# A two-layer linear-attention and gated-MLP kernel on one core: the key weights' transposing load first in SyncE's queue, X's first tile at the head of ScalarE's, and a new order of the operations

## The chip, the cores and the metric

The kernel runs on one core of a Trainium2 chip. Its time is device microseconds of one execution, as the median of three runs: 388.36 us before the change (388.30 to 389.07). Lower is better. The engines are named as in the profile: PE (TensorE, matmuls), PEld (its weight loads), DVE (VectorE), ACT (ScalarE), POOL (GpSimd) and SP (SyncE, which only issues DMAs here). DMAs are issued by SP, whose queue is q1 in the profile, and by ACT, whose queue is q10.

## What is computed

x has 2048 rows of 512 values. The reference applies the same two blocks twice: linear attention with 32 heads of 16, then a gated MLP of width 1376, each on a layer norm of x and added to x.

```python
qkv = x @ wqkv                                  # q, k, v: 32 heads of 16
pq = einsum("bhsd,hdf->bhsf", q, w_phi)         # and pk from k
phi_q = concat([softmax(pq), softmax(-pq)])     # and phi_k from pk
kv = einsum("bhsf,bhsd->bhfd", phi_k, v)
z = einsum("bhsf->bhf", phi_k)
o = (phi_q @ kv) / (phi_q @ z + 1e-6)
x = x + o @ wo                                  # on layernorm(x)
x = x + (relu(gate) * up) @ W_down              # gate, up on layernorm(x)
```

## The kernel before

x stays in SBUF as X, 16 tiles of 128 rows, four tiles to a chunk. For each tile of the first layer norm DVE takes statistics (`bn_stats`, L311, and `bn_aggr`, L313), POOL makes the scale and the bias from them (L319 to L370), ACT, DVE or POOL normalises (L382 or L394), and the result is turned, so that the 512 columns lie on partitions: by a DMA that transposes, issued by SP (L412 for one tile, L408 for two), or by PE (L403) with a copy out of PSUM (L405). Tile 0 is turned by PE in layer 0.

The weights of q and k are folded with w_phi once (`feature_weights`): wkT, the key weights turned, comes by one transposing DMA straight out of DRAM (L169). DVE spreads w_phi into Wblk (L269), PE multiplies (four folds of four matmuls, L287), and ACT and DVE copy the four results into Wk2 (copies are recorded at L249 for ACT and L251 for DVE). The query weights follow later in the same way (their turn is L279 on SP).

Then comes, for each tile of a chunk, the key stage: the key product on PE (L575), two exponentials on ACT (L580), the value product (L516) with its copy to vext, sums over the features on DVE (L546 to L556, partly with POOL, L532), a reciprocal (L589), the scaling on POOL or DVE (L595), and the product that gathers kv and z in PSUM (L617, cleared first by L610). Queries go the same way (L659, L663, L670, L674, L681) and end in a transposing DMA (L683). Attention multiplies by R (L700, built on DVE at L639), divides (L718, L720), turns by PE (L740) or DMA, projects with wo (L751) and adds to X (L420). The MLP is L446 to L498.

PE also runs 18 "wake" matmuls of zeros (L260) whose result nobody reads; where they stand is part of the order.

Nothing is scheduled at run time. `Plan` collects some 1860 operations with a planned cost, and `ORDER` is a list that gives the sequence in which they are emitted; each engine runs its own operations in that sequence and waits where an operand or a buffer isn't ready. `STEP` holds, by characters, which engine does an operation of a tile, and in which form. `WF_IN`, `WK_IN`, `WV_IN`, `WQ_IN` and `X_IN` are the planner's guesses of when the first loads land; they enter only its own arithmetic, by which buffer slots are assigned, and are no waits.

The first loads are issued in `setup` ahead of the plan: SP issues X's tile 0 (L168) and the turn of the key weights (L169); ACT issues w_phi (L170), X's tile 1 (L171), tiles 2 and 3 (L172), then the value weights wvt (L179) and the rest of X (L180 to L182).

Of the kernel before, what the change touches and what calls it, by code (L numbers as in the profile page):

```python
# [133 lines left out]
WF_IN, WK_IN, WV_IN, WQ_IN, LOADED = 3.35, 6.0, 8.3, 13.0, 13.0  # L134
X_IN = [3.1, 4.7] + [6.8] * 2 + [9.8] * 4 + [11.3] * 4 + [12.8] * 4
# [8 lines left out]
def setup(ctx, tc, A_x, A_wqkv, A_w_phi, A_wo, B_W_gate, B_W_up, B_W_down, out):  # L144
    nc = tc.nc
# [16 lines left out]
    X = const.tile([P, T, D], BF16, name="X")  # L162
    xv = xf.rearrange("(t p) d -> p t d", p=P)
# [4 lines left out]
    nc.sync.dma_start(out=X[:, 0:1, :], in_=xv[:, 0:1, :])  # L168
    nc.sync.dma_start_transpose(out=wkT[:], in_=A_wqkv[:, D:2 * D])  # L169
    nc.scalar.dma_start(out=wf[:], in_=A_w_phi.rearrange("(b j) d f -> (j d) b f", b=NDB, j=8))  # L170
# [517 lines left out]
def attention(st, c, pT, norm, L):  # L688
# [257 lines left out]
```

## Time and profile before

| | us |
|---|---|
| median of three runs | 388.36 |
| the profiled execution | 387.81 |
| its span in the trace | 386.1 |
| PE busy in the span | 369.1 |
| DVE busy | 277.5 |
| ACT busy | 195.5 |
| POOL busy | 133.7 |

The span runs from the first to the last recorded instruction. In rows of the timeline the columns are start, duration, engine, line, operation, output and inputs, count, and in brackets the engine's idle time ahead of it with what ended that. In the chain of work that ended last they are start, duration and what. In busy time by stretch they are the stretch, its length, the busy time of PE, PEld, DVE, ACT and POOL with the number of instructions, the granted PE clock as a share, the DMA engines' busy share and GB/s. In rows of a DMA queue they are packets, MB and the time that the packets took as a share of 16 engines.

### The profile page before, as it was taken

How to read it: one execution, taken by the hardware profiler on the slowest of the kernel's cores; microseconds unless marked ns; L12 is line 12 of the kernel's file. 1: busy time of each engine (PE TensorE's matmuls, PEld its weight loads, DVE VectorE, ACT ScalarE, POOL GpSimd, SP SyncE). 2: the span in 40 equal slices, each digit the busy share in tenths (PEclk: the TensorE clock that was granted, in tenths of full speed). 3: DMA queues.
4: the chain of work that ended last, by engine and by line, in shares of the span. 5: the costliest groups of instructions: out<-in, count | busy, mean ns of one | idle time of the engine just before them, and what ended most of it. 6: DMA issues, size and time to landing. Idle time of an engine off the chain costs nothing.

```text
span 386.1 us, 6719 instructions
## 1 busy us (share of the span) xinstructions
PE 369.1 (96%) x2412; PEld 191.1 (49%) x2412; DVE 277.5 (72%) x606; ACT 195.5 (51%) x418; POOL 133.7 (35%) x273
## 2 busy tenths in 40 slices
PE   4799999999989999999999999999999999999997
PEld 1345454666544554444454445476545445444444
DVE  5599999999858786466659878989974565423432
ACT  2689967934456621225876456896443714032100
POOL 4489885832542100053315253451622211000000
PEclk9599999999999999999999999999999999999999
DMA  8679585735582440014203132464793330201004
GB/s 182 186 125 213 136 242 110 124 64 95 112 129 54 83 69 15 0 28 86 48 6 68 28 44 41 82 121 76 129 156 65 67 59 4 54 14 56 0 5 133
DMA packets 100673, 31.95 MB, mean 83 GB/s; under 512 B 92096, under 2 KB 100640, under 8 KB 100640
## 3 DMA queue, kind: packets, MB, share of 16 engines
q1 hardware_dynamic: 97584, 29.02, 38.7%
q10 hardware_dynamic: 3056, 2.51, 2.3%
q8 instruction: 19, 0.31, 0.3%
q14 instruction: 14, 0.11, 0.1%
HBM read 7.39 MB, written 2.10 MB: 25 GB/s over the span
## 4 chain that ended last, share of the span: by engine, by line
PE 75%; DVE 13%; DMA 6%; ACT 2%; issue 2%; POOL 1%; SPq 0%; POOLq 0%
PE ps L466 34%; PE ps L498 17%; PE ps L751 6%; PE ps L659 4%; PE ps L575 4%; DMA b<-b 4%; PE ps L516 3%; PE ps L446 2%; DMA wkT<-in_A_wqkv_dram 2%; DVE sk L556 2%; DVE rk L589 2%; DVE sk L546 2%; DVE sq L546 2%; PE q L700 2%; DVE b L595 1%
## 5 line engine op out<-in xcount | busy, mean ns | idle before, releaser
L476 ACT CAST b<-ps 128x512 bf16<-128x512 f32 (+2 forms) x100 | 47.8, 503 | 99.5 <-PE ps L466 94.4
L466 PE MATMUL ps<-b,wg 128*128 128x512 bf16 (+2 forms) x400 | 79.6, 336 | 0.0
L498 PE MATMUL ps<-wd,b 128*128 128x512 bf16 (+4 forms) x374 | 79.6, 366 | 0.0
L466 PE MATMUL ps<-b,wu 128*128 128x512 bf16 (+2 forms) x400 | 78.8, 336 | 0.0
L479 DVE SCALAR_TENSOR_TENSOR b<-ps,b 128x512 bf16<-128x512 f32 (+2 forms) x70 | 39.9, 604 | 27.7 <-PE ps L466 13.9
L595 POOL TENSOR_TENSOR b<-b,rk 128x1024 bf16<-128x1024 bf16 (+7 forms) x29 | 40.1, 1396 | 43.1 <-ACT b L476 13.1
L498 PEld LDWEIGHTS <-b 128*128 128x128 bf16 (+1 forms) x374 | 35.2, 98 | 38.7
L466 PEld LDWEIGHTS <-wu 128*128 128x128 bf16 x400 | 36.0, 98 | 33.0 <-issue 0.3
L466 PEld LDWEIGHTS <-wg 128*128 128x128 bf16 x400 | 35.9, 98 | 31.4
L424 DVE TENSOR_TENSOR X<-X,ps 128x512 bf16<-128x512 bf16 (+2 forms) x34 | 22.1, 653 | 33.4 <-PE ps L498 23.4
L580 ACT ACTIVATE b<-ps 128x512 bf16<-128x512 f32 x64 | 36.3, 646 | 10.1 <-PE ps L575 10.1
L382 ACT ACTIVATE b<-X,ve,rstd 128x512 bf16<-128x512 bf16 x39 | 32.1, 834 | 15.8 <-POOL ve L370 14.4
L663 ACT ACTIVATE b<-ps 128x512 bf16<-128x512 f32 x64 | 34.2, 615 | 10.7 <-PE ps L659 10.5
L575 PE MATMUL ps<-Wk,b 128*128 128x512 bf16 x128 | 32.9, 387 | 4.4 <-DMA b<-b 2.4
L516 PE MATMUL ps<-wvt,b 128*128 128x512 bf16 x128 | 32.5, 384 | 0.4 <-ACT vext L249 0.4
L751 PE MATMUL ps<-wo,b 128*128 128x512 bf16 x128 | 31.5, 379 | 0.4 <-DMA b<-b 0.4
L681 POOL TENSOR_TENSOR b<-b,rq 128x512 bf16<-128x512 bf16 x23 | 24.6, 1070 | 19.1 <-DVE rq L674 15.6
L659 PE MATMUL ps<-Wq,b 128*128 128x512 bf16 x128 | 30.9, 379 | 0.0
L334 ACT ACTIVATE sq<-X 128x512 bf16<-128x512 bf16 x32 | 20.3, 635 | 18.6 <-DVE X L420 18.4
L420 DVE SCALAR_TENSOR_TENSOR X<-ps,X 128x512 bf16<-128x512 f32 x32 | 21.6, 678 | 5.9 <-PE ps L498 5.1
L341 POOL TENSOR_SCALAR u<-mv 128x2 f32<-128x2 f32 (+1 forms) x20 | 4.6, 234 | 55.8 <-DVE X L420 55.4
L546 DVE TENSOR_REDUCE sq<-b 128x64 f32<-128x1024 bf16 x20 | 23.7, 1201 | 0.0
(86 smaller groups left out, 461.1 us busy)
## 6 DMA issues: line engine op xcount, KB each, us to landing
out_dram<-X SPq DMA_DIRECT2D x15, 128.0 KB, 1.8
X<-in_A_x_dram ACTq DMA_DIRECT2D x3, 512.0 KB, 9.5
b<-b SPq DMA_TRANSPOSE x95, 3.1
wd<-in_B_W_down_dram SPq DMA_DIRECT2D x5, 256.0 KB, 3.3
wu<-in_B_W_up_dram SPq DMA_DIRECT2D x8, 160.0 KB, 3.9
wg<-in_B_W_gate_dram SPq DMA_DIRECT2D x8, 160.0 KB, 3.1
wvt<-in_A_wqkv_dram ACTq DMA_DIRECT2D x1, 512.0 KB, 7.4
wo<-in_A_wo_dram SPq DMA_DIRECT2D x4, 128.0 KB, 3.6
```

The lines of the kernel that those rows point to most:

```text
L466: nc.tensor.matmul(ps[:], lhsT=wt[:, b, f * P:(f + 1) * P], rhs=xnT[:, lo:hi, b, :], start=(b == 0), stop=(b == NDB - 1))
L476: pl.op("ACT", 0.065 + 0.42 * share, lambda ups=ups, ru=ru: nc.scalar.copy(out=ru[:], in_=ups[:]), reads=[(ups, 0)], writes=[(ru, 0)])
L479: pl.op("DVE", 0.08 + 0.53 * share, lambda gps=gps, ru=ru, h=h, cs=cs: nc.vector.scalar_tensor_tensor(out=h[:, cs], in0=gps[:], scalar=0.0 ...
L498: nc.tensor.matmul(yps[:], lhsT=hs[f][:fsz, ti * P:(ti + 1) * P], rhs=st.wd[:fsz, f, cols], start=(f == 0), stop=(f == NFT - 1))
L516: nc.tensor.matmul(vp[:], lhsT=xnT[:, ti, kb, :], rhs=st.wvt[:, kb, :], start=(kb == 0), stop=(kb == NDB - 1))
L546: pl.op("DVE", 1.13, lambda: nc.vector.tensor_reduce(out=sums[:].rearrange("p j s h -> p (j s) h"), in_=e[:].rearrange("p j s (f h) -> p ( ...
L575: nc.tensor.matmul(ps[:], lhsT=xnT[:, ti, kb, :], rhs=w(kb), start=(kb == 0), stop=(kb == NDB - 1))
L580: pl.op("ACT", 0.49, lambda s=s, ek=ek, pk=pk: nc.scalar.activation(out=ek[:, :, s, :], in_=pk[:].rearrange("p (j x) -> p j x", j=8), func ...
L595: eng.tensor_tensor(out=phiK[:, lo:hi, :, :].rearrange("p j s (f h) -> p (j s) f h", h=4), in0=ek[:, lo:hi, :, :].rearrange("p j s (f h) - ...
L659: nc.tensor.matmul(pq[:], lhsT=xnT[:, ti, kb, :], rhs=st.Wq2[:, kb, :], start=(kb == 0), stop=(kb == NDB - 1))
L663: pl.op("ACT", 0.49, lambda s=s, eq=eq, pq=pq: nc.scalar.activation(out=eq[:, :, s, :], in_=pq[:].rearrange("p (j x) -> p j x", j=8), func ...
L751: nc.tensor.matmul(yps[:], lhsT=turned(b), rhs=st.wo[:, b, :], start=(b == 0), stop=(b == NDB - 1))
```

## The change

The two loads on SP become one, and X's tile 0 goes to ACT's queue, ahead of w_phi. The planner's landing times are set anew. Three characters of `STEP` change. `ORDER` is a new list; it has two operations fewer (1861), because with tile 14's second layer norm on DVE (in "xB0") two small POOL operations that fed ACT are not needed. "qs0" moves the scaling of tile 9's query features in layer 0 from DVE to POOL.

```diff
-WF_IN, WK_IN, WV_IN, WQ_IN, LOADED = 3.35, 6.0, 8.3, 13.0, 13.0
-X_IN = [3.1, 4.7] + [6.8] * 2 + [9.8] * 4 + [11.3] * 4 + [12.8] * 4
+WF_IN, WK_IN, WV_IN, WQ_IN, LOADED = 5.5, 5.7, 8.25, 13.0, 13.0
+X_IN = [3.1, 6.0] + [6.75] * 2 + [9.75] * 4 + [11.25] * 4 + [12.75] * 4
...
-    nc.sync.dma_start(out=X[:, 0:1, :], in_=xv[:, 0:1, :])
     nc.sync.dma_start_transpose(out=wkT[:], in_=A_wqkv[:, D:2 * D])
+    nc.scalar.dma_start(out=X[:, 0:1, :], in_=xv[:, 0:1, :])
     nc.scalar.dma_start(out=wf[:], in_=A_w_phi.rearrange("(b j) d f -> (j d) b f", b=NDB, j=8))
...
-    "sB1": 3, "sA": 3, "xB0": "ADADDADDDADADDAD", "xB1": "DADAAADDDAAAADAA", "xA": "AADDDDDAAAAAAAAA",
-    "xm0": "21122111", "xmB0": "12222112", "xmB1": "22222221", "xm1": "11222212", "om0": "11112222",
+    "sB1": 3, "sA": 3, "xB0": "ADADDADDDADADDDD", "xB1": "DADAAADDDAAAADAA", "xA": "AADDDDDAAAAAAAAA",
+    "xm0": "21122111", "xmB0": "22222112", "xmB1": "22222221", "xm1": "11222212", "om0": "11112222",
...
-    "qm1": "DDDDPPDDDDPDDPDD", "qr0": "1111H1122121P1PP", "qr1": "1112112122111112", "qs0": "PPPPPPPPDDDPDPPP",
+    "qm1": "DDDDPPDDDDPDDPDD", "qr0": "1111H1122121P1PP", "qr1": "1112112122111112", "qs0": "PPPPPPPPDPDPDPPP",
```

The lists of `ORDER` are not printed. Engine by engine the sequence differs up to the first attention tiles of layer 0 and is the same behind them but for the two moved operations. What the text on record speaks of:

| engine | before | after |
|---|---|---|
| PE, start | 12 wakes, folds 3, 1, 0, 2, turn of tile 0, keys 0, 3 wakes, values 0, L610, keys 1, values 1 | 8 wakes, folds 3, 0, wake, turn of tile 0, fold 2, wake, fold 1, keys 0, 2 wakes, values 0, 4 wakes, L610, values 1, keys 1 |
| ACT, start | copies of folds 0, 1, 2, normalise tile 1, copy of the turned tile 0, normalise 2, 3, exponentials of tile 0 | copies of fold 0, turned tile 0, folds 2, 1, normalise tiles 1, 2, exponentials of tile 0, normalise 3 |
| DVE, ahead of the first key sum (L556, tile 0) | statistics of tiles 0 to 8 | of tiles 0 to 7; tile 2's ahead of the copy of fold 3 |
| DVE, ahead of the sum of tile 1 (L546) | statistics of tiles 0 to 11, 13, 15 | and of tile 14; the aggregate of tile 15 comes later |
| DVE, ahead of the first L720 | 104 operations | the same and one reciprocal of tile 5 (L670) |
| PE, ahead of the first L740 | 94 operations | the same and L700 of tile 1 |
| SP, behind the turn of tiles 6 and 7 | turn of tiles 8 and 9, then weight loads | two weight loads, then the turn of tiles 8 and 9 |

186 rows, old and new, of the table ORDER are left out of this document.

## The prediction

> **What bounds the kernel now.** I read the page first, then busy time by stretch, then the chain of work that ended last, then the timeline of single engines. The page and the stretches say where time can be won at all:
>
> ```profile
> span 386.1 us, 6719 instructions
> PE 369.1 (96%) x2412; PEld 191.1 (49%) x2412; DVE 277.5 (72%) x606; ACT 195.5 (51%) x418; POOL 133.7 (35%) x273
> ...
> 0.00:20.00 20.00, 12.27 (x47) 5.46 (x48) 11.33 (x34) 8.94 (x14) 9.61 (x35) 0.74 0.75 178
> 20.00:40.00 20.00, 19.69 (x123) 9.48 (x121) 19.77 (x40) 18.72 (x36) 18.30 (x24) 1.00 0.85 172
> 40.00:60.00 20.00, 18.68 (x175) 10.27 (x174) 20.00 (x38) 16.18 (x33) 16.98 (x13) 1.00 0.71 186
> ...
> 120.00:160.00 40.00, 40.00 (x215) 19.49 (x214) 28.95 (x54) 14.71 (x30) 4.05 (x10) 1.00 0.24 40
> ```
>
> PE is busy 369.1 of 386.1 us; 7.7 us of its 17.0 idle us lie in the first 20. From 20 to 60 DVE is full (19.77 and 20.00 of 20), so there DVE sets the pace. From 120 on it is PE alone. The chain says the same with the places:
>
> ```profile
> 1.24 9.20 DMA wkT<-in_A_wqkv_dram
> ...
> 10.48 1.47 PE ps L287 x12
> ...
> 14.73 0.05 issue
> 14.78 1.89 PE ps L575 x4
> 16.67 1.28 PE ps L260 x3
> ...
> 19.35 0.33 PE q L610 x2
> 19.68 0.97 PE ps L575 x4
> 20.65 0.88 PE ps L516 x4
> ...
> 63.70 0.60 DVE b L720
> ...
> 64.35 0.40 PE ps L740 x4
> ```
>
> First the DMA of wkT until 10.44 (1.24 + 9.20), then folding, the first key product at 14.78, PE until 21.5, from 23.4 to 64.3 DVE, and from the first attention's transposes (L740, 64.35) PE. DVE's own timeline has these waits from 5 to 64 us, and one ahead of a copy of Wk:
>
> ```profile
> 7.82 1.29 DVE L311 BATCH_NORM_STATS2 bnst<-X 128x6 f32<-128x512 bf16 x2 [2.13 <-DMA X<-in_A_x_dram]
> ...
> 11.73 1.87 DVE L311 BATCH_NORM_STATS2 bnst<-X 128x6 f32<-128x512 bf16 x3
> ...
> 17.82 0.69 DVE L556 TENSOR_REDUCE sk<-b 128x32 f32<-128x512 bf16 x1 [2.82 <-ACT b L580]
> ...
> 23.37 1.22 DVE L546 TENSOR_REDUCE sk<-b 128x64 f32<-128x1024 bf16 x1 [0.23 <-ACT b L580]
> ```
>
> So what the change wins it wins through the moment at which DVE begins its unbroken run, the key sum of tile 0 at 17.82, and through what it has done by then.
>
> **Part 1: the loads.** SP issues X's tile 0 at 0.79 and the turn of the key weights at 1.24; afterwards the turn is issued at 0.79 and tile 0 goes ahead of w_phi on ACT's queue.
>
> ```profile
> 0.79 0.39 SPq L168 DMA_DIRECT2D X<-in_A_x_dram  x1
> 1.24 3.00 SPq L169 DMA_TRANSPOSE wkT<-in_A_wqkv_dram  x1
> ...
> q1 hardware_dynamic: 12, 0.00, 5.4%
> ...
> 21.47 2.18 SPq L279 DMA_TRANSPOSE b<-in_A_wqkv_dram  x1
> ...
> q1 hardware_dynamic: 54, 0.01, 28.5%
> ...
> q10 hardware_dynamic: 363, 0.37, 110.4%
> ```
>
> The q rows are DMA by stretch: SP's queue (q1) moved its first 12 packets of wkT from 3.0 to 3.25, some 1.8 us after its issue. The same turn for the query weights, issued at 21.47, had its first 54 packets from 22.8 to 23.0 (none in the 0.4 us before): 1.33 us. With nothing ahead wkT should start at 0.79 + 1.33 = 2.1 in place of 3.0. Bounds for the landing: 0, if the shared engines finish it when they finish it now, and -1.8, if all of that start went (1.8 sooner would also give 386.5, the low end below). From 8 to 9 only ACT's queue (q10) moved bytes, so wkT's data were through by 8 and its end, seen at 10.44, came behind the other queue's bytes: that is the reason for the end at 0. I take -0.9, from the query weights' row: landing at **9.54**.
>
> The Trainium skill ("DMA: Bandwidth & Descriptors", Issuing engines are not separate DMA queues) says that DMAs of all issuing engines run on the same 16 DMA engines and interleave, and that spreading them saves only issue time. It speaks against this part: by it the landing would gain 0.45 and the sum would be -0.48, 387.9; no row here shows either yet.
>
> The other loads get one issue (0.39) later on ACT. X's tiles 2 and 3 land by 7.82 now; DVE would wait for them ahead of the Wk copy, which is due at about 10.2, so up to 1.4 us (their statistics take 0.6 and 0.3) is covered. w_phi has cover until 9.5.
>
> **Part 2: the order from the landing to DVE's run.** Before, from landing to first key product: 14.78 - 10.44 = 4.34 us: four folds, three Wk copies on ACT, the normalise of tile 1, then the copy of the turned tile 0. Afterwards PE does fold, fold, wake, turn of tile 0, fold, wake, fold, and ACT's normalise of tile 1 comes behind all four copies.
>
> ```profile
> 10.48 1.89 PE L287 MATMUL ps<-Wblk,wkT 128*128 128x128 bf16 x16 [4.51 <-DMA wkT<-in_A_wqkv_dram]
> 12.16 0.63 PE L403 MATMUL ps<-ident,b 128*128 128x128 bf16 x4
> ...
> 12.94 0.60 ACT Wk L249
> ...
> 16.70 1.08 ACT L580 ACTIVATE b<-ps 128x512 bf16<-128x512 f32 x2 [0.57 <-PE ps L575]
> ...
> 8.68:12.09 3.41, 1.61 (x16) 1.61 (x17) 1.61 (x5) 0.11 (x1) 2.08 (x7) 0.50 1.10 334
> 12.09:15.51 3.42, 1.44 (x9) 0.72 (x8) 2.91 (x8) 3.42 (x7) 0.97 (x4) 0.50 0.57 178
> 15.51:18.92 3.41, 3.41 (x9) 1.21 (x8) 1.10 (x4) 2.39 (x4) 1.42 (x4) 0.50 0.57 114
> 18.92:22.33 3.41, 3.41 (x17) 1.40 (x16) 3.41 (x9) 2.09 (x5) 3.04 (x6) 1.00 0.34 77
> ```
>
> At this half clock: folds 4 x 0.49 (1.47 over three) = 1.96, wakes 2 x 0.43 (1.28 over three) = 0.86, turn 0.42 (from the folds' end at 12.37 to 12.79), start 0.04; then the last copy 0.60 and two hops of 0.05: 3.98 us. Of the 18 wakes 8 run ahead of the folds in place of 12, which costs nothing there, since PE idles until wkT lands (4.51). The two among the folds cost 0.86, the normalise that left gives most of that back, and the first fold's and turn's copies hide behind PE. From product to exponential is 1.92 (14.78 to 16.70), from there to DVE's sum 1.12. Run start: 9.54 + 3.98 + 1.92 + 1.12 = 16.56 against 17.82, **-1.26**.
>
> Less is done by then. One tile's statistics (1.87/3 = 0.62) come behind the first sum and one small aggregate (0.1) ahead of it. Ahead of the first attention's L720 stands one reciprocal more (0.3, below), and the 0.23 wait goes: -1.26 + 0.62 - 0.10 + 0.30 - 0.23 = **-0.67** at 64.3. PE has then done one more product of attention (0.26, tile 1's L700, covered by the wait for DVE), so it has 0.26 less to do: **-0.93**.
>
> That holds if tile 1's second exponential is there when DVE wants it, at about 23. Keys 0 start at 13.52; two wakes, values 0, four wakes, L610, values 1 and keys 1 follow. This hangs on the clock. The windows show it at half until 18.92, through 1.61 and 1.44 busy us of 3.41, and full after a stretch with 3.41. Afterwards PE would be busy about 2.5 us of the first stretch and 2.8 of the second. I take it that 2.8 suffices: full at 15.51. Then keys 1 end near 19.7, and DVE's run sets the pace.
>
> The Trainium skill ("TensorE: Matmul & The Clock Gate", Part 1) says that the window is free-running, some 3.4 us long, and that a busy one releases the clock. The rows agree with the length; how busy is enough no run here shows.
>
> **Part 3: the rest of the order and STEP.** Tile 9's query scale goes from DVE (0.42) to POOL (1.05), tile 14's second normalise from ACT to DVE, and two small POOL operations vanish. The character changed in xmB0 belongs to a pair that is normalised singly and does nothing.
>
> ```profile
> L681 POOL TENSOR_TENSOR b<-b,rq x10: 1050/1051/1053, 59.5 to 100.5; 128x512 bf16<-128x512 bf16 x10
> L681 DVE TENSOR_TENSOR b<-b,rq x4: 363/422/426, 85.0 to 108.6; 128x512 bf16<-128x512 bf16 x4
> ...
> 90.53 1.05 POOL L681 TENSOR_TENSOR b<-b,rq 128x512 bf16<-128x512 bf16 x1 [2.94 <-DVE rq L674]
> ...
> ...
> L670 DVE RECIPROCAL sq<-sq 128x32 f32<-128x32 f32 x32 | 10.1, 330 | 0.1
> ```
>
> POOL waited 2.94 us ahead of its neighbour, and the normalise lies where PE is 40.00 of 40 busy: 0, covered. If the cover is gone, 1.05 - 0.42 = 0.6. On SP two weight loads (issue up to 0.57 each) now stand ahead of the turn of tiles 8 and 9.
>
> ```profile
> 28.82 0.57 SPq L242 DMA_DIRECT2D wd<-in_B_W_down_dram  x1
> ...
> 35.70 1.04 PE L575 MATMUL ps<-Wk,b 128*128 128x512 bf16 x4 [0.30 <-DMA b<-b]
> ```
>
> PE already waited 0.30 for such a turn; DVE uses those keys much later. Cost between 0 and 2 us of PE; I take 0, since PE's waits from 20 to 60 sum to 1.6 us (0.31 and 1.32, from the first fence) while DVE sets the pace.
>
> **Sum.** -0.93 on the profiled execution, 387.81 (span 386.1), which is below the median of the runs, 388.36. Against the median: **387.4**. A difference under 0.2% (0.78 us) is about what a measurement of this kernel can't tell from none.
>
> **The rivals.**
> - *Clock unchanged* (full at 18.92, as now). Keys 0 end at 15.24, wakes 16.10, values 0 at 17.82, four wakes 19.24, L610 19.5, values 1 and keys 1 (0.88 each) 21.25; exponential, value copy, exponential: tile 1's sum at 23.2, against 23.37. With tile 14's statistics moved ahead (-0.62), 0.4 of aggregate and reciprocal, and 0.26 of PE: -0.65, 387.7. For it: only a full stretch has released it in this trace.
> - *Clock still earlier* (12.09, on 2.5 busy us): keys 0 some 0.9 sooner, -1.8, 386.5. Against it: 1.61 did not do.
> - *Landing unchanged*, since both queues' bytes share the engines, and the clock too: run start 10.44 + 7.02 = 17.46, -0.36 + 0.59 = +0.23, less 0.26: 388.3, no change; with the 0.45 of issue 387.9. For it: q10 alone from 8 to 9. Against it: the query weights' turn starts sooner with nothing ahead.
> - *Clock a window later* (22.33), the slower side: from 17.8 the four wakes take 1.72, L610 0.5, values 1 1.72, keys 1 some 1.2, to 23.0; tile 1's sum at 24.8 in place of 23.37: +1.45 - 0.62 + 0.4 - 0.26 = +1.0, 389.4. It decides if PE stands more than a fraction of the stretch from 15.5 to 18.9; the same mechanism, a sum that waits for its exponential anywhere in DVE's rewritten run, turns to slower from 1.7 us of such waits (0.93 + 0.78). For it: DVE's run has only 0.23 of waits now, so the new order can hardly have fewer. Against it: six wakes fill that stretch.
>
> **How the numbers follow.** Chances: forecast 0.35, clock unchanged 0.18, still earlier 0.12, landing unchanged 0.10, slower 0.25. The forecast lies close to the bound, so a third of it counts as no change, as does most of the clock-unchanged case. Faster 0.40, same 0.32, slower 0.28. Range from the earlier clock, 386.5, to the slower case, 389.4.
>
> **What would show it.** wkT lands near 9.5; first key product near 13.5; full clock from a stretch with under 3.41 busy us; DVE's run from near 16.6 with waits under 0.5 to 64; L740 near 63.7; PE as long as now after that. I am wrong if wkT lands at 10.4, if DVE's run has gaps of its own, or if PE's waits after 64 grow.

## The result, and the profile after

The changed kernel takes 384.05 us (median of four runs, 383.55 to 384.49) against 388.33 us for the kernel before in the same session (386.84 to 389.07): a ratio of 0.9894, 95% interval 0.9861 to 0.9927. It is faster by about 4.3 us, and the time lies below the forecast range. The profiled executions are 384.49 us against 387.81, a difference of 3.3 us; their spans differ by 3.6. They are two single executions, so what follows reads their stages, not their difference to a tenth.

The page and the stretches of the changed kernel (columns as in the rows of before):

```profile
span 382.5 us, 6719 instructions
PE 367.4 (96%) x2412; PEld 190.8 (50%) x2412; DVE 277.2 (72%) x606; ACT 195.3 (51%) x417; POOL 133.4 (35%) x272
```

```profile
0.00:20.00 20.00, 16.04 (x73) 7.41 (x74) 15.72 (x44) 12.59 (x22) 13.13 (x41) 1.00 0.78 199
20.00:40.00 20.00, 18.33 (x136) 9.51 (x135) 19.52 (x37) 19.43 (x39) 17.56 (x21) 1.00 0.89 170
40.00:60.00 20.00, 17.73 (x157) 9.42 (x156) 18.91 (x35) 14.98 (x30) 15.28 (x12) 1.00 0.70 146
...
120.00:160.00 40.00, 40.00 (x216) 19.46 (x214) 27.28 (x51) 13.63 (x27) 3.48 (x8) 1.00 0.23 40
```

The gain is made in the first 20 us: PE is busy 16.04 us there against 12.27, DVE 15.72 against 11.33. Between 20 and 60 a part is given back: DVE, which was full before (19.77 and 20.00), is now busy 19.52 and 18.91 of 20, and PE loses 1.36 and 0.95 us too. The chain of work that ended last has another beginning, and another course behind it:

```profile
1.21 4.43 DMA wf<-in_A_w_phi_dram
...
5.74 0.77 DVE Wblk L269 x2
...
6.65 1.01 PE ps L287 x8
...
10.47 1.02 PE ps L575 x4
...
19.09 0.99 ACT b L580 x2
...
22.94 4.88 DMA b<-b
27.87 1.04 PE ps L575 x4
...
55.91 4.95 DMA b<-b
```

The long piece was the turn of the key weights (9.20 us, until 10.44). Now it is the load of w_phi (wf), 16 KB, until 5.64. The first key product (L575) starts at 10.47 in place of 14.78. The first attention's transposes (L740), where PE takes over, start at 61.33 in the same chain (64.35 before). In between the chain no longer follows DVE. Of the stretch from 12 to 61 us DVE holds 2.5 us of it, where it held 33.1 before; the rest runs over ACT, two turns by DMA (4.88 and 4.95 us), PE and POOL. The first of these two is that of tiles 8 and 9, which now stands on SP behind two weight loads (issued at 21.75 and 22.39 us).

The timeline of the changed kernel shows why the turn no longer decides, and DVE's run:

```profile
0.79 1.41 SPq L168 DMA_TRANSPOSE wkT<-in_A_wqkv_dram  x1
...
5.74 0.76 DVE L269 TENSOR_TENSOR Wblk<-M,wf 128x256 bf16<-128x256 bf16 x2 [1.37 <-DMA wf<-in_A_w_phi_dram]
...
12.83 0.69 DVE L556 TENSOR_REDUCE sk<-b 128x32 f32<-128x512 bf16 x1
...
30.18 1.22 DVE L546 TENSOR_REDUCE sk<-b 128x64 f32<-128x1024 bf16 x1 [0.48 <-ACT b L580]
...
47.25 0.69 DVE L556 TENSOR_REDUCE sk<-b 128x32 f32<-128x512 bf16 x1 [1.09 <-ACT b L580]
```

The turn's issue is recorded with 1.41 us (3.00 before). The DMA view gives it 5.2 us from issue to landing (9.2 before), so it is there at 5.99 in place of 10.44. DVE's run starts 4.99 us earlier (12.83 for 17.82), but has two waits for ACT's exponentials, 0.48 and 1.09 us, where it had 0.23.

### The profile page after: what moved, and what is told of

The parts are those of the page before. It is cut to its first block, busy times and chain, and to the rows that moved or that the text cites. A ratio compares the mean times of both kernels' runs of the same rounds, so it can differ in the third digit from the quotient of the medians.

```text
span 382.5 us, 6719 instructions
## 1 busy us (share of the span) xinstructions
PE 367.4 (96%) x2412; PEld 190.8 (50%) x2412; DVE 277.2 (72%) x606; ACT 195.3 (51%) x417; POOL 133.4 (35%) x272
## 3 DMA queue, kind: packets, MB, share of 16 engines
q10 hardware_dynamic: 3200, 2.64, 2.4%
## 4 chain that ended last, share of the span: by engine, by line
PE 77%; DMA 7%; DVE 6%; ACT 5%; POOL 3%; issue 1%; ACTq 0%; POOLq 0%; DVEq 0%
PE ps L466 35%; PE ps L498 16%; PE ps L751 6%; DMA b<-b 6%; PE ps L575 5%; PE ps L659 5%; PE ps L516 4%; PE ps L446 3%; PE q L700 2%; ACT b L580 2%; DMA wf<-in_A_w_phi_dram 1%; DVE sk L556 1%; ACT b L382 1%; PE q L617 1%; ACT vext L249 1%
## 5 line engine op out<-in xcount | busy, mean ns | idle before, releaser
L382 ACT ACTIVATE b<-X,ve,rstd 128x512 bf16<-128x512 bf16 x38 | 31.1, 829 | 15.5 <-POOL ve L370 14.0
L575 PE MATMUL ps<-Wk,b 128*128 128x512 bf16 x128 | 32.3, 379 | 6.1 <-DMA b<-b 4.1
L681 POOL TENSOR_TENSOR b<-b,rq 128x512 bf16<-128x512 bf16 x24 | 25.6, 1070 | 15.7 <-DVE rq L674 12.0
L546 DVE TENSOR_REDUCE sq<-b 128x64 f32<-128x1024 bf16 x20 | 23.7, 1202 | 0.0
```

What stands on the lines that cost most here:

```text
L382: pl.op("ACT", 0.72, lambda to=to, t=t, j=j: nc.scalar.activation(out=to(), in_=st.X[:, t, :], func=AF.Identity, scale=rstd[:, j:j + 1], b ...
L575: nc.tensor.matmul(ps[:], lhsT=xnT[:, ti, kb, :], rhs=w(kb), start=(kb == 0), stop=(kb == NDB - 1))
```

## The experiments

Each run is one edit of the kernel before or of the changed kernel. "Old order" is the `ORDER`, `STEP` and constants of before; "new order" those of the changed kernel. Landing is the turn's issue plus its time to landing; the distance is the span less the start of the first key product. Traces are single executions, medians are of 4 to 10 runs, each ratio is to the kernel before in the same session.

| run | order | landing | first key product | span | distance | median | ratio (95%) |
|---|---|---|---|---|---|---|---|
| before | old | 10.44 | 14.78 | 386.1 | 371.3 | 388.33 | 1 |
| e1 | old | 5.99 | 11.24 | 382.1 | 370.9 | 383.69 | 0.9877 (0.9845-0.9909) |
| e5 | old | 6.29 | 12.49 | 383.5 | 371.0 | 384.50 | 0.9900 (0.9863-0.9936) |
| e6 | old | 9.49 | 13.88 | 384.5 | 370.6 | 385.57 | 0.9939 (0.9920-0.9958) |
| e7 | old | 6.93 | 10.89 | 380.2 | 369.3 | 382.74 | 0.9863 (0.9827-0.9898) |
| e11 | old | 6.93 | 11.37 | 382.0 | 370.6 | 383.56 | 0.9874 (0.9842-0.9905) |
| e12 | old | 12.99 | 17.32 | 387.4 | 370.1 | 390.60 | 1.0062 (1.0039-1.0086) |
| e13 | old | 12.50 | 16.81 | 387.1 | 370.3 | 390.04 | 1.0052 (1.0026-1.0077) |
| e14 | old | 5.28 | 10.77 | 381.1 | 370.3 | 382.59 | 0.9860 (0.9824-0.9897) |
| after | new | 5.99 | 10.47 | 382.5 | 372.0 | 384.05 | 0.9894 (0.9861-0.9927) |
| e2 | new | 12.03 | 15.92 | 387.6 | 371.7 | 389.57 | 1.0029 (1.0001-1.0057) |
| e3 | new | 5.89 | 13.86 | 386.2 | 372.3 | 387.89 | 0.9990 (0.9967-1.0013) |
| e4 | new | 7.34 | 11.19 | 383.6 | 372.4 | 385.61 | 0.9918 (0.9887-0.9949) |
| e8 | new | 5.79 | 9.70 | 381.4 | 371.7 | 384.05 | 0.9896 (0.9865-0.9928) |
| e9 | new | 5.79 | 10.05 | 382.0 | 371.9 | 384.54 | 0.9900 (0.9862-0.9937) |
| e10 | new | 6.53 | 10.24 | 382.1 | 371.9 | 385.25 | 0.9915 (0.9885-0.9946) |
| e15 | new | 5.98 | 10.57 | 383.1 | 372.5 | 384.72 | 0.9903 (0.9877-0.9929) |

The table has a simple shape: the end follows the first key product. Its start varies by 7.6 us, the distance behind it by 3.2, and that mostly by the order: 369.3 to 371.3 in the old one, 371.7 to 372.5 in the new one. A part of this difference lies in the start itself: with the same loads the first key product comes 0.2 to 0.8 us earlier in the new order (e1 and after, e7 and e10, e14 and e15).

**e1: the loads alone.** The kernel before with the two lines of `setup`.

```diff
-    nc.sync.dma_start(out=X[:, 0:1, :], in_=xv[:, 0:1, :])
     nc.sync.dma_start_transpose(out=wkT[:], in_=A_wqkv[:, D:2 * D])
+    nc.scalar.dma_start(out=X[:, 0:1, :], in_=xv[:, 0:1, :])
```

> The old order with the new loads. Theory (the loads carry the gain, the clock goes with them): wkT lands near 6.0 us, the folds start between 6.0 and 6.8, PE's clock stays full from then on, and the time is 384.2 to 385.5 us. Rival (the new order is needed to use the early landing): wkT lands as early, but the time stays above 386.5 us.

383.69 us, below the forecast: the two lines carry the whole gain. The clock did not go with them, the first key product ran at half speed (1.89 us), and the folds began at 7.58 us, later than forecast.

**e2: the order alone.** The changed kernel with the two load lines as before (the diff above, reversed).

> The new order with the old loads. Theory (the loads carry the gain): wkT lands near 10.4 us and the time is 387.5 to 389.0 us, as before. Rival (the new order is worth more than 1 us by itself): at most 387.0 us.

389.57 us, so the rival is out: the order alone gains nothing, and is slower by 0.3%, at the edge of what the interval tells. In its trace the turn also landed later (12.03 us), with the same loads as before.

**e3: X's tile 0 back to SP, behind the turn.**

```diff
     nc.sync.dma_start_transpose(out=wkT[:], in_=A_wqkv[:, D:2 * D])
-    nc.scalar.dma_start(out=X[:, 0:1, :], in_=xv[:, 0:1, :])
+    nc.sync.dma_start(out=X[:, 0:1, :], in_=xv[:, 0:1, :])
```

> The new order; SP issues the turn of the key weights first and X's tile 0 second, ACT has w_phi, tile 1, tiles 2 and 3 as in the kernel before. Theory A (the turn is slow because ACT's plain loads run beside it): wkT lands between 8 and 10 us, since tile 1 and tiles 2 and 3 come as early as before. Rival B (it was slow because tile 0 stood ahead of it in SP's queue): wkT lands near 6.0 us. Time by A 386 to 388.5, by B 383.5 to 385.

The turn landed as early as in the changed kernel (5.89 us), so that isn't owed to the tile's place on ACT's queue. On the landing rival B came true: ACT issued its loads as early as before, and moved as many packets beside the turn, but the turn got more through. DMA from 4 to 5 us of the kernel before, then of e3:

```profile
q1 hardware_dynamic: 518, 0.13, 85.1%
q10 hardware_dynamic: 58, 0.06, 28.4%
```

```profile
q1 hardware_dynamic: 957, 0.24, 107.7%
q10 hardware_dynamic: 63, 0.05, 15.1%
```

So the loads beside the turn aren't the whole reason for its length. The time, 387.89 us, lies in theory A's range, but not by A's mechanism: the tile now came late. The timeline of e3:

```profile
2.26 0.62 SPq L169 DMA_DIRECT2D X<-in_A_x_dram  x1
7.70 0.69 DVE L311 BATCH_NORM_STATS2 bnst<-X 128x6 f32<-128x512 bf16 x1 [4.94 <-DMA X<-in_A_x_dram]
8.97 0.75 DVE L269 TENSOR_TENSOR Wblk<-M,wf 128x256 bf16<-128x256 bf16 x2
```

DVE waits 4.94 us for the tile, and Wblk, which the folds need, stands behind that in DVE's sequence. The folds began at 9.87, four us after the turn had landed. Moving the tile to the head of ACT's queue is thus the second half of the edit: it keeps the tile early.

**e4: the old loads, but ACT's loads of X from tile 1 on, and wvt, held back behind its first activation.** In the new order.

```diff
-    nc.scalar.dma_start(out=X[:, 1:2, :], in_=xv[:, 1:2, :])
-    nc.scalar.dma_start(out=X[:, 2:4, :], in_=xv[:, 2:4, :])
...
-    nc.scalar.activation(out=wake[:], in_=st.zero[:, 0:1], func=AF.Exp)
+    nc.scalar.activation(out=X[:, 1:16, 0], in_=st.zero[:, 0:15], func=AF.Exp)
+    nc.scalar.copy(out=wvt[:, 0, 0:1], in_=X[:, 3, 0:1])
+    nc.scalar.dma_start(out=X[:, 1:2, :], in_=xv[:, 1:2, :])
+    nc.scalar.dma_start(out=X[:, 2:4, :], in_=xv[:, 2:4, :])
```

> The new order; SP has tile 0 and then the turn, as before the change, but ACT issues w_phi alone early and the rest of X and the value weights only behind its first activation, from about 4 us. Theory A (loads beside the turn): wkT lands between 6.2 and 7.0 us although tile 0 is ahead of it. Rival B (tile 0 ahead of it): 9 us or later. The time is no verdict here, since X comes about 2 us later; by A I expect 384.5 to 387.

With the tile still ahead of it and its issue still long (2.64 us), the turn landed at 7.34 us, between the two forecasts, 3.1 earlier than before and 4.7 earlier than in e2, which has the same order. Taking away either one shortens the turn: the load ahead of it (e3, 5.1 us from issue to landing) or the plain loads beside it (e4, 6.1), against 9.20 with both. DMA by stretch, first of the kernel before from 3 to 8 us, when both queues ran, then of the changed kernel from 2 to 5 and from 6 to 10 (packets, MB and share, as in the rows of before; on the first line the mean rate):

```profile
DMA packets 2518, 0.97 MB, mean 195 GB/s; under 512 B 2080, under 2 KB 2518, under 8 KB 2518
...
q1 hardware_dynamic: 2048, 0.52, 74.4%
q10 hardware_dynamic: 470, 0.45, 38.7%
```

```profile
DMA packets 2815, 0.74 MB, mean 246 GB/s; under 512 B 2624, under 2 KB 2815, under 8 KB 2815
...
q1 hardware_dynamic: 2080, 0.52, 79.4%
q10 hardware_dynamic: 735, 0.21, 36.7%
```

```profile
DMA packets 1407, 1.39 MB, mean 348 GB/s; under 512 B 48, under 2 KB 1407, under 8 KB 1407
...
q10 hardware_dynamic: 1407, 1.39, 110.2%
```

Before, the turn (q1, 0.52 MB) takes 5 us beside 0.45 MB of ACT's loads, and the two together move 195 GB/s. After, it goes through in 3 us beside 0.21 MB, at 246 GB/s, and then X's tiles go alone at 348. In the turn's own packets that is 410 a us against 693. One behind the other would have been sooner than the mixed stretch, by an estimate from rows: at 715 packets a us, the rate of the query weights' turn with ACT's queue silent (shown further below), 2048 packets take 2.9 us, and 0.45 MB at 348 GB/s take 1.3, together 4.2 us and not 5. But the sum doesn't always fall. In e12, below, both queues together move 359 GB/s from 10 to 11 us, and the turn still gets only 289 packets a us:

```profile
DMA packets 581, 0.36 MB, mean 359 GB/s; under 512 B 303, under 2 KB 581, under 8 KB 581
...
q10 hardware_dynamic: 292, 0.28, 81.7%
q1 hardware_dynamic: 289, 0.07, 32.8%
```

The Trainium skill ("DMA: Bandwidth & Descriptors", Queues, rings and completion order) says that each DMA engine alternates between the queues it has work for, packet by packet. The stretch of e12 agrees with that (292 and 289 packets); the mixed stretch before the change doesn't show it (470 and 2048).

**e6 and e7: what a load ahead of the turn does.** Both are e1, the turn issued at the same moment (1.19 and 1.23 us), once with a load of 32 bytes ahead of it on SP, once with nothing ahead but a wait for DVE (its line moves down from the head of `setup`).

```diff
+    nc.sync.dma_start(out=tiny[:], in_=xv[0:1, 0, 0:16])
     nc.sync.dma_start_transpose(out=wkT[:], in_=A_wqkv[:, D:2 * D])
```

```diff
     nc.vector.memset(st.zero[:], 0.0)
+    nc.vector.memset(wkT[:, 0, 0:1], 0.0)
+    nc.sync.dma_start_transpose(out=wkT[:], in_=A_wqkv[:, D:2 * D])
```

> The old order with the new loads, and a load of 32 bytes ahead of the turn in SyncE's queue; X's first tile stays on ScalarE's. Theory Q (whatever stands ahead in the queue delays the turn): its issue takes about 3 us again, its first packets come after 3 us, it lands 8.5 us or more after its issue, and the time is 387 to 388.5 us. Rival S (it is the 128 KB of X's tile ahead of it that count): only the tiny load's issue of about 0.45 us is lost, the turn lands 5 to 5.6 us after its issue at 1.24, near 6.5 us, and the time is 383.7 to 384.5 us.

> The old order with the new loads; the turn stays first in SyncE's queue but waits for a short write of VectorE into its destination, so that it is issued near 1.3 us instead of 0.79, when ScalarE's loads are already on their way. Theory Q (the place in the queue counts): the issue takes about 1.4 us, the turn lands 5.2 us after it, near 6.5 us, and the time is 383.7 to 384.6 us. Rival L (what counts is to be ahead of ScalarE's loads): the issue takes near 3 us or the packets run at the old pace, it lands after 9 us and the time is 387 to 388.5 us.

The DMA issues of e6, then of e7 (the last figure is us from issue to landing):

```profile
wkT<-in_A_wqkv_dram SPq DMA_TRANSPOSE x1, 8.3
```

```profile
wkT<-in_A_wqkv_dram SPq DMA_TRANSPOSE x1, 5.7
```

The turn lands 8.3 us after its issue against 5.7, and the times are 385.57 and 382.74 us. Rival S of e6 is out (it had 5 to 5.6), and theory Q is nearly right on the landing (it had 8.5 or more) but not on the way there: the issue took 1.74 us and not 3, the first packets came before 3 us, and the time is lower than it had. Rival L of e7 is out, and its time is lower than theory Q had. Set in a row, the landing goes from 10.44 (before) to 9.49 (128 KB ahead become 32 bytes), 6.93 (nothing ahead) and 5.99 (issued 0.44 earlier).

**e12 and e13: the same pair, later.** The write on which the turn waits stands behind that of vext, so that the turn is issued at 2.8 us; e12 with the 32 bytes ahead, e13 with nothing ahead.

```diff
     nc.vector.memset(st.vext[:, :, :, DH:DH + 1], 1.0)
+    nc.vector.memset(wkT[:, 0, 0:1], 0.0)
+    nc.sync.dma_start_transpose(out=wkT[:], in_=A_wqkv[:, D:2 * D])
```

> The old order with the new loads, 32 bytes loaded first on SyncE's queue, and the turn held back to about 2.85 us, when the small load has landed. Theory P (the turn is slowed by a load that is still on its way on the same queue): issue 1.4 us, landing 5.0 to 6.0 us after the issue, near 8.3 us, and the time is 384.5 to 386 us. Rival N (it is slowed by not being the queue's first transfer at all): landing 8 us or more after the issue, beyond 10.8 us, and the time is 387 us or more.

> The old order with the new loads; the turn is the first transfer of SyncE's queue but held back to about 2.8 us by a short write of VectorE, as in the run with the small load ahead of it, here with no load ahead. Theory N (not being its queue's first transfer is what slows it): issue 1.4 us, landing 5.0 to 6.5 us after the issue, near 8.5 us, first key product near 12.6 us, time 385 to 386.5 us. Rival T (issued as late as 2.8 us it is slow because ScalarE's loads are under way): issue over 3 us, landing 9 us or more after it, near 12 us or later, time over 388.5 us.

e12 alone seemed to speak for rival N, e13 refutes it (theory N there): first in its queue, with an issue of 1.42 us, the turn still took 9.7 us. ACT's large loads (wvt and X's later tiles, 512 KB each) are issued from the same moment on, 2.79 us, and the turn's first packets come only after 6, when those are under way. From 8 to 12 us e13 shows both queues at once again:

```profile
q10 hardware_dynamic: 1010, 1.00, 79.2%
q1 hardware_dynamic: 944, 0.23, 31.3%
```

So being first in the queue is not enough here: the turn must be through before the large loads run. In the changed kernel the first of them is issued at 3.03 us, and the turn's packets have all gone by 5.

**e14: the turn first on the other queue.** Old order; the turn on ACT, the four small loads on SP.

```diff
     nc.sync.dma_start(out=X[:, 0:1, :], in_=xv[:, 0:1, :])
-    nc.sync.dma_start_transpose(out=wkT[:], in_=A_wqkv[:, D:2 * D])
-    nc.scalar.dma_start(out=wf[:], in_=A_w_phi.rearrange("(b j) d f -> (j d) b f", b=NDB, j=8))
-    nc.scalar.dma_start(out=X[:, 1:2, :], in_=xv[:, 1:2, :])
-    nc.scalar.dma_start(out=X[:, 2:4, :], in_=xv[:, 2:4, :])
+    nc.scalar.dma_start_transpose(out=wkT[:], in_=A_wqkv[:, D:2 * D])
+    nc.sync.dma_start(out=wf[:], in_=A_w_phi.rearrange("(b j) d f -> (j d) b f", b=NDB, j=8))
+    nc.sync.dma_start(out=X[:, 1:2, :], in_=xv[:, 1:2, :])
+    nc.sync.dma_start(out=X[:, 2:4, :], in_=xv[:, 2:4, :])
```

> The old order; the turn is the first transfer of ScalarE's queue at 0.79 us, and SyncE's queue takes X's first tile, w_phi, X's second tile and tiles 2 and 3 in that order. Theory N (first transfer of its queue, whichever that is): issue 1.4 us, landing near 6 us, first key product 10.8 to 11.5 us, time 383.2 to 384.6 us. Rival S (SyncE's queue itself serves the turn best, or the plain loads issued at the same instant come first): landing after 8.5 us, time over 386.5 us.

Landing at 5.28 us and 382.59 us (382.33 to 382.87), the lowest median of all runs, with e7 at 382.74: it is no property of SP's queue. Both are some 1.4 us below the changed kernel, with intervals that overlap its own. The Trainium skill ("DMA: Bandwidth & Descriptors", Silent corruption: two transposing streams in flight at once) warns of transposing DMAs of two queues in flight together. Here the first one on SP is issued at 10.26 us, five us after this one has landed; a version built on e14 has to keep it so.

**e5: w_phi ahead of X's tile 0 on ACT**, since w_phi ends last in the changed kernel. An edit of e1, in the old order.

```diff
-    nc.scalar.dma_start(out=X[:, 0:1, :], in_=xv[:, 0:1, :])
     nc.scalar.dma_start(out=wf[:], in_=A_w_phi.rearrange("(b j) d f -> (j d) b f", b=NDB, j=8))
+    nc.scalar.dma_start(out=X[:, 0:1, :], in_=xv[:, 0:1, :])
```

> The old order with the new loads, and w_phi issued ahead of X's first tile on ScalarE's queue. Theory (the first key product sets the end one for one): w_phi lands by 4.5 us instead of 5.65, the folds begin at the key weights' landing, about 6.1 us instead of 7.58, the first key product falls near 9.8 us (11.24 with X's tile first), and the time is near 382.3 us (383.69). Rival (the folds' evacuations or X's later tiles set the first key product): it stays at 10.8 us or later and the time within 0.4 us of 383.7. Second rival: X's first tile, now later, holds VectorE ahead of the masked w_phi, and the time is 383.7 to 384.7 us.

384.50 us: the second rival. The timeline of e5:

```profile
5.08 0.69 DVE L311 BATCH_NORM_STATS2 bnst<-X 128x6 f32<-128x512 bf16 x1 [2.32 <-DMA X<-in_A_x_dram]
...
6.35 0.42 DVE L269 TENSOR_TENSOR Wblk<-M,wf 128x256 bf16<-128x256 bf16 x1
...
8.21 1.87 PE L287 MATMUL ps<-Wblk,wkT 128*128 128x128 bf16 x16 [2.80 <-DVE Wblk L269]
```

w_phi landed 2.2 us after its issue, at 3.0, but tile 0 came late: DVE waits 2.32 us for it and takes its statistics at 5.08 (3.16 in e1). They stand ahead of Wblk on DVE, and the folds began at 8.21 instead of 7.58 in e1. As in e3, what must be early is the last of the three loads that the folds need.

**e8, e9 and e11: what the wake matmuls and the clock are worth.** e8 (new order) and e11 (e7's kernel) cut all 18 wakes to one column, e9 (new order) the last ten.

```diff
-    nc.tensor.matmul(z[:], lhsT=st.zero[:, 0:P], rhs=st.zero[:], start=True, stop=True)
+    nc.tensor.matmul(z[:, 0:1], lhsT=st.zero[:, 0:P], rhs=st.zero[:, 0:1], start=True, stop=True)
```

> The changed kernel with its 18 opening matmuls cut to one column each (their result is used by nothing), so that TensorE does not count as busy ahead of the folds: what the clock is worth. Theory (the full clock at the folds and the first key products is a small part of the gain, as the kernel with the new loads alone had half of it for 6.8 us and was no slower): granted clock half from the start until some 15 to 20 us, first key product about 0.8 us later than 10.47, time 384.5 to 385.7 us. Rival (the clock is most of the gain): first key product 2 us later or more, time over 386.5 us.

> The changed kernel with the first 8 opening matmuls whole and the other 10, which lie between the folds and the first value products, cut to one column (their result is used by nothing). Theory (the kernel's end follows its first key product at a fixed distance of about 372 us in the new order): the folds run through without the three matmuls between them, the first key product comes near 9.7 us instead of 10.47, at the same clock as in the changed kernel, and the time is 383.0 to 383.6 us (384.05 for the changed kernel). Rival (other waits between 12 and 61 us take it back): the first key product is earlier and the time within 0.3 us of 384.05.

> The old order with the new loads and the turn held back, and all 18 opening matmuls cut to one column (their result is used by nothing). Theory C (that run was faster than the one without the wait because TensorE was at its full speed at the first key products): four folds and key products take twice as long as there until some 13 us, the distance from the first key product to the end grows from 369.3 to 370.5 us or more, and the time is 383.7 to 385 us (382.74). Rival (the clock at the start is hidden): within 0.4 us of 382.74.

In e8 the first key product comes earlier, at 9.70, and runs at half speed; the median is that of the changed kernel. e9's first key product is earlier too (10.05), and its time shows nothing of that beyond its interval. e11 is 0.8 us above e7, and their intervals overlap. The times of e8 and e9 fell to neither forecast, that of e11 between its two. By these medians the clock at the start is worth something between nothing and 0.8 us.

**e10 and e15: the new order with the two best sets of loads**, that is e7's and e14's `setup` in the changed kernel.

> The changed kernel, its turn held back to about 1.25 us by a short write of VectorE into its destination, as in the run with the old order that gave 382.74 us. Theory O (the old order, not the loads, is what made that run the best): the turn lands near 6.95 us and w_phi near 4.1, the folds begin at 6.95 to 7.1 (6.65 in the changed kernel), and the time is 384.0 to 384.7 us. Rival (holding the turn back helps by itself, through the earlier w_phi): 382.4 to 383.2 us.

> The changed kernel's order and constants with the loads of the fastest run (the turn first on ScalarE's queue, X's first tile, w_phi, tile 1 and tiles 2 and 3 on SyncE's). Theory (the new order costs something behind the first key product, about 1 us, by new waits of VectorE and TensorE between 12 and 61 us): first key product 10 to 10.5 us, no later than the 10.77 of the old order, distance from it to the end of the span 371.7 to 372.3 us (370.3 in the old order), time 383.4 to 384.6 us against 382.59. Rival (the orders are worth the same): 382.2 to 383.0 us.

385.25 against 382.74, above both forecasts, and 384.72 against 382.59, 0.1 us above the theory's. Busy time by stretch of e14 and then of e15 (PE, PEld, DVE, ...):

```profile
20.00:40.00 20.00, 18.84 (x129) 9.19 (x130) 20.00 (x36) 19.44 (x39) 18.49 (x22) 1.00 0.81 169
40.00:62.00 22.00, 19.73 (x179) 10.80 (x182) 22.00 (x44) 15.77 (x33) 16.06 (x13) 1.00 0.75 191
```

```profile
20.00:40.00 20.00, 18.16 (x130) 9.29 (x129) 19.52 (x35) 19.29 (x37) 17.92 (x23) 1.00 0.87 165
40.00:62.00 22.00, 19.23 (x170) 10.03 (x169) 20.74 (x40) 16.26 (x33) 16.32 (x15) 1.00 0.73 157
```

In the old order DVE never stops (20.00 and 22.00); in the new one it loses 0.48 and 1.26 us. The waits of e15 name what it waits for (us in total, times, longest):

```profile
DVE sk L556 <- ACT b L580: 1.3, 1, 1.3
DVE sk L546 <- ACT b L580: 0.5, 1, 0.5
```

They are the same two waits as in the changed kernel. The chains say more. In all nine traces of the old order DVE holds 33 to 42 us of the chain that ended last between 12 and 61 us, in all eight of the new one 2.5 to 10.4 us; there ACT holds 11 to 21 us, and PE's key products wait 1.7 to 3.3 us in all for turns of tiles by DMA (0 to 1.3 in the old order).

With before and e2, and e1 and the changed kernel, there are four pairs that differ in the order alone; the new order is the slower one in each (by 1.0 us in e2's session, where the turn also landed later, then 0.4, 2.5 and 2.1). Each pair alone is close to its interval, but in the last two every run of the new order is slower than any of the old one. The distance of the table, without overlap over 17 executions, points the same way: 372.05 against 370.5 in the mean, of which the earlier start is a part. So the new order costs something behind the first key product, between 0.4 and 2.5 us by the pairs.

## Why the prediction was wrong, step by step

- **What bounds the kernel.** Right for the kernel before, and the end followed the first key product in every run. But the forecast let DVE's run set the pace after the change too, and there it doesn't: between 12 and 61 us the chain holds 2.5 us of DVE, and runs over ACT and the turns by DMA.
- **The landing, -0.9 (bounds 0 to -1.8).** This is the step that failed: -4.45 (10.44 to 5.99). The start was right, 2.1 us (the turn's packets run from 2 us on, as the stretch from 2 to 5 shows). The error was to move the end by as much as the start. That took the length of the transfer for given, while it hangs on what stands ahead of it on its queue and on what runs beside it: 9.20 us with both, 5.1 in e3, 6.1 in e4. The row that I read as the reason for no gain (ACT's queue alone from 8 to 9) didn't bind: after the change ACT's queue runs alone from 5 on, and the landing came at 5.99. The trace of before had the other length as well: the query weights' turn, of which I used the start alone, had ACT's queue silent beside it and took 5.1 us from issue to landing. DMA of the kernel before from 23 to 24 us, and that issue:

```profile
q1 hardware_dynamic: 715, 0.18, 93.7%
...
b<-in_A_wqkv_dram SPq DMA_TRANSPOSE x1, 5.1
```

That is 715 packets a us against 410 a us (2048 in 5 us) of the key weights' turn. By this rate the 2048 packets take 2.9 us from 2.1 on, so that the data would be through by 5.0, as they were. That it fits so well is partly luck: the rate wasn't even, SP's queue moved only 38 packets from 24.3 to 25.2 us, ahead of that turn's landing at 26.6. From there to the landing another 1.0 us passed, where it was 2.4 before (8 to 10.44, with 32 more packets of SP's queue between 9 and 10); I had no term for that.
- **The rule of the Trainium skill** beside this step, that spreading loads saves only issue time (0.45 us, 387.9), was no bound here: e1 saves 4.9 us (388.60 for the kernel before in its session) with the same bytes on the same two queues. Its first half agrees with the traces, the transfers do interleave.
- **w_phi has cover until 9.5.** True only for a turn that lands there. With the turn at 5.99, w_phi (5.64, and Wblk by 6.5) ends last, and the folds begin 0.66 us after the turn's landing, at 6.65.
- **From landing to first key product, 3.98 us.** Right: 3.82 from the folds' start (6.65 to 10.47).
- **The clock.** My three rivals hung on it, with prices of 0.3 to 2 us. In e8 and e9 no such price shows, in e11 one of 0.8 us that its interval doesn't tell from none. In the changed kernel the folds ran at half speed as assumed, and the key product at full speed, where half was assumed.
- **DVE's run, -0.67 at 64.3 with waits under 0.5.** Its start moved by -4.99, L740 by -3.02. So some 2 us of the gain were lost in between. The waits of 0.48 and 1.09 us are most of that, and one tile's statistics (0.62, by the prediction) that come later; but L740 no longer follows DVE in the chain, it follows a turn by DMA that lands at 60.86 us. The mechanism of the slower rival, a sum that waits for its exponential in the rewritten run, did happen; it needed over 1.7 us of waits and got about 1.6, against a gain at the landing five times that of the forecast.
- **Part 3 and the order, 0 (bounds 0.6, and 0 to 2 us of PE).** The order costs 0.4 to 2.5 us behind the first key product by the four pairs, within the bounds that I gave and did not choose. The place that I put at 0, the turn of tiles 8 and 9 behind two weight loads, is on the changed kernel's chain (issued at 22.94, landed at 27.82, and PE waits 0.52 us for it). No run moves those two loads back, and none undoes the three characters of STEP alone, so what the rest of the sequence costs isn't told apart from them.

**What stays open.** Why 32 bytes ahead of the turn delay it by 2.6 us when ACT's loads are issued at the same moments up to 2.8 us (e6, e7) was not found. The recorded issue was longer (1.74 for 1.41 us); whether that is cause or sign, no run tells. Nor was it found why the turn of e3, with nothing ahead of it, got more packets through beside as many of ACT's. The landings are single executions: with the same loads the turn landed at 10.44 in before and 12.03 in e2.

## What to carry to other kernels

A transfer's length in a trace is its length with what stood ahead of it and ran beside it: before moving a load, look for a stretch in which a transfer of the same kind ran alone, and take its rate from there. At the start of a kernel the load that the first dependent work waits for goes first, with nothing ahead of it on its queue, and the large loads of the other queue come late enough for it to be through. An order that was tuned around a late operand is to be measured again on its own when the operand comes early: here the two load lines alone, with the old order, were as good as the whole change or better.

## What the runs showed of the hardware

- A transposing DMA of 512 KB went at 410 packets a us beside plain loads (before, 3 to 8 us), at 693 with few beside it (after, 2 to 5), at 715 with none (before, 23 to 24) and at 289 in e12 from 10 to 11. Together the two kinds moved 195, 246 and, in e12, 359 GB/s; plain loads alone moved 348.
- The recorded issue of one and the same transposing DMA of 512 KB was 1.41 or 1.42 us in twelve traces with nothing ahead of it on its queue, and 1.74 to 4.27 us in the five with something ahead (1.74 in e6, 2.64 in e4, 2.98 in e2, 3.00 before, 4.27 in e12).
- The granted clock of PE as the profile shows it can miss its speed near the start. The timeline of e8 has the first key products at half speed, four in 1.87 us (1.02 in the changed kernel), and the stretch that holds most of them is given as 1.00:

```profile
9.70 1.87 PE L575 MATMUL ps<-Wk,b 128*128 128x512 bf16 x4 [0.81 <-ACT Wk L249]
```

```profile
10.00:13.00 3.00, 3.00 (x15) 1.23 (x14) 2.82 (x9) 2.56 (x5) 1.90 (x6) 1.00 0.97 275
```

The Trainium skill ("TensorE: Matmul & The Clock Gate", Part 1) calls the trace's clock events unreliable at times; in e8 the mean duration of a matmul tells more than that column.
